# Set attention with a SwiGLU feed-forward on one core: the same instructions in another searched order

## The chip, the cores and the metric

The kernel runs on one core of a Trainium2 chip. Its engines work side by side, each through its own list of instructions in order: TensorE (PE, matmuls; PEld is its weight load), VectorE (DVE), ScalarE (ACT), GpSimd (POOL), and SyncE (SP), which here does nothing but issue transfers (DMAs). Matmul results land in one of eight PSUM banks and everything else lives in SBUF. The metric is the device time of one execution in microseconds; the figure for a kernel is the median of its runs.

## What is computed

Four batches of 12416 tokens with 128 channels. A first attention lets 32 learned vectors look at all tokens of a batch; a second lets every token look at the 32 results; the outcome goes through a root-mean-square norm and a gated feed-forward of width 1536.

```python
def mab(q, kv):
    s = scale * (q @ kv.transpose(0, 2, 1))
    s = s - s.max(-1, keepdims=True)
    a = np.exp(s)
    a /= a.sum(-1, keepdims=True) + 1e-09
    return a @ kv
h = mab(I, x)
return mab(x, h).astype(np.float32)
...
rms = np.sqrt(np.mean(x * x, axis=-1, keepdims=True) + 1e-06)
xn = x / rms * rms_g
g = xn @ w_gate
silu = g * (1.0 / (1.0 + np.exp(-g)))
val = xn @ w_val
return (silu * val @ w_out).astype(np.float32)
```

## The kernel before

**Tiling.** A batch is cut into seven sets of tokens (five of 2048, one of 1920, one of 256). The sets are cut into units of 512 tokens (480 in the sixth set, 256 in the seventh), 25 units a batch and 100 in all. A unit has 12 blocks, one for each 128 of the 1536 hidden columns: 1200 blocks.

**One block.** The token's output of the second attention is a mix of 32 vectors, so the two input products of the feed-forward are done on the 32 weights of the mix: a tile `a` of 128 rows (high, low, high, low halves of the weights) against a stack `sg` or `sv` of the 32 vectors already multiplied by `w_gate` or `w_val`. The letters are those of the order below.

- g: the gate matmul (line 655, PE). s: silu of it (line 665, ACT). v: the value matmul (line 683, PE). m: their product (line 697, DVE).
- Then the product with `w_out`, in one of three kinds. A block of kind P does it as one plain matmul p in full precision (line 753, PE, two instructions). Kinds S and D split the number in a high and a low part and use three faster matmuls: h (high part, ACT, line 710 for S, 707 for D), the low part l (line 716, DVE) for S, or n (line 723, POOL) and e (line 729, ACT) for D, then q (two matmuls, lines 741 and 742), d (the sum of both parts, line 761, POOL), and r (the third matmul, line 753).
- When a unit's 12 blocks are through: E scales up the first sum into an output buffer (line 785, ACT), F adds the second (794, DVE), T transposes (800, DVE) and O stores, as four transfers of 64 KB (line 813, SP). There are two output buffers, so E of a unit needs the store of the unit two before to have landed.

**Transfers on SP's queue.** Beside the stores: a *gather* (letter a, line 593) brings a unit's tile `a` together by four transfers of 64 KB; a *strip* (`load_channels`, line 110) loads a quarter of the channels of one set of the next batch, 256 KB in pieces of 128 bytes (32 KB for the seventh set); *rows* (`load_rows`, line 99) load one set of the next batch, four transfers; a *placement* (`place`, line 479) puts a part of a new stack in place, three transfers; `fetch` (line 458) and `put` (line 197) move weights. SP issues them strictly one after the other, and waits where one needs data or a buffer.

**The attention of the next batch** runs between the blocks of this one: strips are turned (line 300, DVE), scored (317, PE), exponentiated, summed (369, PE) and so on, each step a "micro" with a number.

**The order.** Nothing decides an order at run time. The prologue (about the first 48 us) is written out in ORDER. All that follows is in strings that an offline search wrote: `program` has one letter for each step (a dot stands for the next micro in `taken`), `picks` says which of the waiting blocks a step takes, `sorts` gives each block's kind, and `banks`, `workers`, `holders` say which buffer each result gets. Each step is emitted in that order, so the string fixes the order of every engine's own list; between engines, only data and buffers make an instruction wait.

```python
for name in "".join(program.split()):
    if name == ".":
        step, args = micros[int(next(taken))]
        step(*args)
    else:
        do[name]()
```

Of the kernel before, what the change touches and what calls it, by code (L numbers as in the profile page):

```python
# [23 lines left out]
def kernel(  # L24
# [12 lines left out]
    m = inducing.shape[0]  # L37
# [1086 lines left out]
    def seams():  # L1124
# [16 lines left out]
        0234567012456720415671260712036170236170261702367103267037127126342764132643026107243074207230427032043204235405  # L1141
        2431530523105231063506342502314217465762752615721067421074127412043413217643706423064250341530145014350231075423
        0477535436054074237037406326437603726371670527632561073607653146743674651475143261310413411271203406127654015704
        2510275140124713250152145361062102530275015617205742017451426154647626132652361253123610317562043654123742673574
        5145675360471640154012074250765172527521503565167106076754105106170647135631405316450610612064154217450465765104
        6047063710436714631062712613631734254172042104320614306120612014326042135046253035760376273657032465324763453764
        3451370163401543064216520162064506751674607643057603640345304715076013631206431046230463476140641424652014260412
        3640124651263526534253573754123657345713451350135175617210761036251036501635103650346103415317563147642714267316
        4762064201601645124564254135405364727502542304604206740634762317462317415717424571342730530132173267025723052304
        3704571475340345017430753257032734503750350375746041650160316730256736731710573463613563514364625463456147532143  # L1150
        7453253042570325637543604263476342072104720471406152076510460714273021476124716504651761261206417346724361452143
        2162570617031207507302751427043724034130132016430240145607145640714670541765146754073652043507347307235340376506
        7063065367501367163704754617563524635432164317451745067156714507410640536471357137451435132534721653762143123216
        3012346012640361503615436156415634765317650467530670346256042062305625140652165271650716506503265321562060236026
        5042012431653453425215275142710725017261275402743250327304267240720475605671403754630574307326073567326342021370
        4613064130643514210410345130724352351732513463672367526475236520365043201532613562316730563020362736470473020420
        7467354035741074645736054305436204725325305607513753051473156730163517436713512371235126031637401567013547130413
        0714107237523471246521635164312063105436024672473162307362703576025062107620516720162125710351235135013201430450
        3712543572357347632743521726746543105376453643026705674654756745074651065104527146250457641573652315421426052352
        0152017524723475307274236206706273217601467301602043207464053650325435262301051454313501345176504753050370435705  # L1160
        2704572347603504520456123053451361031401675017046720572640720627065472043640764106134017545364130140763073627160
        2357251231507234713574132737215761456421651650624652174602740741074176701731473107306742160264216401502143546513
        0425045674170450140673543145014750750251205145171460742601421624631460146321470216706401676547057154256120521542
        6415624652162345203530543275367035723576235165170527026742057624572104627407250172571520135702351025606350135203
        654135017645076514
    """
    workers = """
        2102102102102102011201021201010101012012012012112120201202020202020120120120120102101201212101201201201201201201
        201
# [5 lines left out]
        abcdefghicebjkflmadnogcbfpqrslmhjndikealcgjbpofhqmarnjpdfhgafsobdcljgprnqkamshfclnbdpgieojfrkqmalspchienofbgadrl  # L1175
        fhdqjipscnmdkoiehaqbcrjgfpnclkesmhoqcfpaernlgisbmhkeodjqpifsolakbdfpmrcshenjkqfbldpoanmrikjesgclhfqpdobsckafengr
        mdjscoqkelpabirhmcodkijlprseafhnqmsprojlbgnkqcoamedsplhfjrmgqindofeklsabmpjcnhrqgosbdkigmlenjrgqkoefhnbcsmaqrpld
        konficqjrsmpkhngreoasqlbmdnfickposqrgjmnhaeilkcgbnafdejhlmoifcdkpqserjnghobfcdelmaknqropigasjdkfalcqabmnerokpshq
        jdimbsngaekihrolfqpdjhscerdsamgcljeqobknhispfrlmcbshiejbqdarigelkpofnjbqsrmhieplkqrgbadnhoemcpjilrsnfbgkaqdmiohc
        gslmecpoknrslqfjcipmbgdraohesfbkjinprmgdbclqsaekjiclogqrdbnmsplifahbecgkqdabojsnhpclaredfbgkmhslnaigfdqporkbnmec  # L1180
        jdiqselocghkrqaenfbjkcerlgbiemqcdnpsejhfadokrlbjsgifmcbarhnedgfqjiosmkflbpigaqrnhfecomdjslknbqgclodrmnjbrcaphkmf
        ebiqnglsojrdkfebgamcpiqlmnoskhcjebgcpqbosmjclnrkipqgfemodahbrcipkesdgjrhamiceglsqdbnphcjfgaemrkobhlihqnmbesrgald
        jkmhcloefsgdiqpanrmcbejlkhnfedabisojgelmqnrkdpiscaoljqbhmdrfagnpkmbojidhfrlqscogebfinjeqpckfodibralmqsgohiedrbaq
        skplncjfmogarhlicqeskpjmfdgolnrahqcgpeobimjnrpqskdalmjnrophfqsecgbkliaprjdoqsnmehkigcolsnjfahkgbcpmrsqiejcdbfkoa
        gnhqbepilmrsfkopaqdrgelkimjfnsqobplchdkfembjikacqdnfehrsmcpgeknaoljmbhqrfdahipkgjscenofbqldaiefprmncbjkhogfsphbc
        dqmroagnjiksfperlobhniaqjmfcrkghdpsnlcmfaeohderkcqjpsbonilhmgecafbqjlrdkpmhionesdqcgbiklajpfrmeioshnkqdgarbcflhj
        moqepncgiaflkrchdbjslfpmagehcrnbjlskidfohrqpbaecfsoidhjkglpmrnqcilahnjqfkbgdmcshrqienkomplfbesrjoqpiangcfkhelqms
        jdiebcklmajfnibrcgskdqmponhegrbqdiajlpemcfskorqjbgdnifmoaphrbslqgenfrjkaidepcikmarhdobsnfgqlkjpeidmrsnakqhlopcgj
        fmebagdkshlnqbamhoeiprlgjcmfdksqniomhbljgckapfrsbqeblphfgnkirqdbomgjlesnkrcahfdgiobpqjeklhsocnmarkgflsndpbmhojcp
        ifnqarekbglmcdofsjpinhlarqgscjlomkrgnpbdjfiqsglaeokhnbdpqmjilcgdfreoiasnlbogfpadclrmhbskeijpqodafgclbjcrspkqemod  # L1190
        filhrnapjgdibqsmkloepbmjfhcdaelgqoimrjpdclsfbqgnhiemodkjrlacqnfsdkicrpbmselokfqhrgpajmdncqkirebpsldifjmgroanpqei
        bkjhlscqgacnpmkdifbrjlhcsneomlabqrkocgpsdmnlijckefpqsmnlkhdbgeijoprnaksqcfhjoipgedrhqlfncpiabgksmfjerdagpoimnfkb
        hsqrclighjprfdlekcmorasnjhdmpiqrbskdojncaflghibodskemqnphijlocbrsekadnfbgemphoqjlndersfkmhbcgopienfahdrcjsbgopkl
        mnaejqiormgbihfkbscajpnfolqmiasdnjrgecqphomflskbnarihqjdfkohnlrbsfeigpcmkdaghqrjpdbsncmoeahfqlirjkbegqihcmsrpakn
        qleomrdsfkeqarcosnkqhlroibg
# [3 lines left out]
        SDDPSSPSSPSPSPSDSSSPSSSSSSPSDPSSSDSSSDSSPSSSSSSPDSSSSPSSDSPSSSPSDPPSSSSDSSSSSSSSSSSDSPSSDSDSSSSDPSSSSDSPPSSPPSSD  # L1199
# [4 lines left out]
        PPSPPSDSDPSSPDSPSSDSPSDSDPPSSDPSSDSSSSSPSDSPDSPSSSPSPPSSPSSPSSSSDDPPPDSSSSDSSSSSPDSSSSDSSSSSPSSSPSDPDSSSPPSDSSSS  # L1204
        SSSSSDSSSPSSPDSSSSDSSSDPSPSDPPSSSPSPSDSPDSSPSPSSDPSSSDSSPSSPPSDSSSSSPPSSPDSPSDSPPPPDSSSSSSPSPPSPSSDSSPSPSSPSDSSS
        SSSSSSPSSDSDPPPSDSSPDSDPSSPSSSPSSDPSSDSPPSSPSSSSSSSPSPSSPDSSDSSSPSPSSDSSSSSSSPSSPPSSPSPSSPDSSSSSSDSPSPSSSSPSDSSS
        PDSPSDPDSSPSPSPSSSSSSPSSPSSSSSSSDSSSPPSSSDSDSSSSPSSPSDSPDPSSPSSPSPSSSSSPSSDSSPDSSPSSSPSSSSSDPSSDSPPSSPSDSSSPPSSP
        SSPSDSSSPSSPSDSSPSSSSPDSSSSSPDSSPSSDPSSDSPSPPPSPSSPSDPPSPDSSSPPSSSPSDSSSSSSSSSSS
    """
    picks = """  # L1210
        CDBCAAABBBABAABBAAAABABAAAAABAAAAAAAAAAAAAAAACACAAAAAAAACBAACAAABBAAACBAABABAAAAACABAABABBAAAABCBABAABBAAABAAAAA
        AAABAAAAAAAAAAABAAAAAAAAAAABAAAAAAAAAAAABAAAAAABAAAAAAAAAAAAABAAAAAAAAAAAAABAAAAAAAACABBBBABACAAAAAABAAAAAAAAAAA
        AAAAAABAAAAABAAAAAAAAACAAAAAAAADBABACAAAAAABBABAAAAABAABCAABAAAAAAAAAAAAABAABBBAABAACAAAABBAAABAAAAAAABAACBCDAAA
        BAACAAAAAADABADAABADABACAAABAAAAAAADABBBABABBAAABAAABBBAABABAACABBBABAAAAAAAABBAABAAAAABABAAAAAABABBAABAADAABAAA
        BBABAAAACAAACBAABBBAAABACABBBBCBAAAABAABBAABABABAAAABCBAACABAAAABAAAAAAAAABAAAAAAAABBBBBAAACAACAAABBBBAABBAAAAAA
# [234 lines left out]
```

## Time and profile before

| | |
|---|---|
| median of three runs | 1524.27 us (1522.7 to 1526.77) |
| the profiled execution | 1520.86 us, span 1518.8 us |
| mean granted clock of TensorE | 0.994 |
| DMA | 112.56 MB, 388592 packets on SP's queue, mean 74 GB/s |
| strips, from issue to landing | 5.5 us median (60 of 256 KB) |
| gathers, from issue to landing | 2.0 us median (156 + 156 of 64 KB) |

The page gives busy time by engine, 40 equal slices of the span, and the chain of work that ended last. Windows cut the span where one likes and give busy time by engine in each; the timeline lists instructions in order of time, with neighbours of one form merged; the waits say who waited for whom. The costliest groups on PE, DVE and POOL (busy time, mean of one, idle time before):

```profile
L655 PE MATMUL gv<-a,sg 128*128 128x512 f32 (+2 forms) x1188 | 507.4, 428 | 12.3 <-DMA a<-lo 9.2
L697 DVE TENSOR_TENSOR gv<-silu,gv 128x512 f32<-128x512 f32 (+2 forms) x681 | 445.5, 668 | 15.8 <-ACT silu L665 7.7
L761 POOL TENSOR_TENSOR u<-xn,u 128x512 fp32r<-128x512 f32 (+2 forms) x327 | 401.6, 1239 | 10.9 <-PE gv L742 10.1
```

Matmuls are pipelined, so their durations overlap and the sum of a group is more than the time that it holds PE; the chain's shares are the better price.

### The profile page before, as it was taken

The numbers are of one execution on the slowest core, as the hardware profiler recorded it, in microseconds if no ns is written. First come the engines' busy times: TensorE is split into PE (matmuls) and PEld (weight loads), VectorE is DVE, ScalarE is ACT, GpSimd is POOL, SyncE is SP. The second block draws the span as 40 slices with busy tenths as digits, with TensorE's granted clock in tenths as the row PEclk, the third lists the DMA queues.
The fourth block names the chain that finished last, engine by engine and source line by source line (L and its number), as shares of the span: only waits on it lengthen the run. The fifth ranks groups of instructions, "written<-read, shape, count | busy, mean of one in ns | idle before, by whom it ended". The sixth has DMA issues, their size and how long they took to land.

```text
span 1518.8 us, 26130 instructions
## 1 busy us (share of the span) xinstructions
PE 1492.1 (98%) x7198; PEld 1107.9 (73%) x7198; DVE 1454.5 (96%) x2572; ACT 1327.1 (87%) x2748; POOL 1426.9 (94%) x1351
## 2 busy tenths in 40 slices
PE   9998999999999999999989999999999999999998
PEld 6556677777776777776768776777678777777786
DVE  6998999999999999999979999999999999999998
ACT  5797899898898889988879888989899989899896
POOL 1497999999999999999989999999999999999998
PEclk9999999999999999999999999999999999999999
DMA  7584225532755213736573222264222112212222
GB/s 290 81 114 85 45 55 124 129 78 49 105 94 98 38 30 63 149 73 108 90 128 62 48 42 43 43 137 100 43 40 43 31 36 42 35 36 43 42 41 34
DMA packets 389329, 112.56 MB, mean 74 GB/s; under 512 B 365088, under 2 KB 369728, under 8 KB 386624
## 3 DMA queue, kind: packets, MB, share of 16 engines
q1 hardware_dynamic: 388592, 110.83, 38.3%
q8 instruction: 57, 0.93, 0.3%
q14 instruction: 88, 0.72, 0.2%
q10 hardware_dynamic: 592, 0.08, 0.0%
HBM read 53.95 MB, written 27.00 MB: 53 GB/s over the span
## 4 chain that ended last, share of the span: by engine, by line
PE 92%; SPq 3%; DVE 2%; ACT 1%; DMA 1%; issue 1%; POOL 0%; DVEq 0%; ACTq 0%; POOLq 0%
PE gv L753 28%; PE gv L655 17%; PE gv L683 16%; PE gv L741 12%; PE gv L742 12%; PE gv L317 3%; SPq L110 2%; PE gv L526 1%; PE gv L369 1%; PE gv L854 1%; DMA a<-lo 1%; SPq L593 0%; DMA xT<-in_x_dram 0%; ACT silu L665 0%; PE gv L153 0%
## 5 line engine op out<-in xcount | busy, mean ns | idle before, releaser
L665 ACT ACTIVATE silu<-gv 128x512 f32<-128x512 f32 (+2 forms) x1193 | 686.4, 590 | 105.8 <-PE gv L655 73.4
L655 PE MATMUL gv<-a,sg 128*128 128x512 f32 (+2 forms) x1188 | 507.4, 428 | 12.3 <-DMA a<-lo 9.2
L697 DVE TENSOR_TENSOR gv<-silu,gv 128x512 f32<-128x512 f32 (+2 forms) x681 | 445.5, 668 | 15.8 <-ACT silu L665 7.7
L683 PE MATMUL gv<-a,sv 128*128 128x512 f32 (+2 forms) x1188 | 455.8, 409 | 4.3 <-ACT o L785 4.3
L761 POOL TENSOR_TENSOR u<-xn,u 128x512 fp32r<-128x512 f32 (+2 forms) x327 | 401.6, 1239 | 10.9 <-PE gv L742 10.1
L761 POOL TENSOR_TENSOR xn<-xn,xn 128x512 fp32r<-128x512 f32 (+2 forms) x309 | 384.9, 1255 | 4.8 <-PE gv L742 4.1
L710 ACT ACTIVATE xn<-gv 128x512 fp32r<-128x512 f32 (+2 forms) x598 | 345.7, 587 | 26.4 <-DVE gv L697 18.8
L697 DVE TENSOR_TENSOR u<-silu,gv 128x512 f32<-128x512 f32 (+2 forms) x512 | 335.6, 665 | 10.3 <-PE gv L683 4.5
L753 PE MATMUL gv<-u,wo 128*128 128x512 f32 (+1 forms) x648 | 326.0, 587 | 0.2
L655 PEld LDWEIGHTS gv<-a,sg 128*128 128x128 f32 x1188 | 225.0, 190 | 121.6 <-issue 31.4
L683 PEld LDWEIGHTS gv<-a,sv 128*128 128x128 f32 x1188 | 223.9, 189 | 96.4 <-issue 21.2
L716 DVE SCALAR_TENSOR_TENSOR xn<-xn,gv 128x512 fp32r<-128x512 f32 (+2 forms) x330 | 216.6, 661 | 7.9 <-ACT xn L710 6.5
L716 DVE SCALAR_TENSOR_TENSOR u<-xn,gv 128x512 fp32r<-128x512 f32 (+2 forms) x268 | 172.9, 650 | 2.1 <-ACT xn L710 0.9
L761 POOL TENSOR_TENSOR xn<-xn 128x512 fp32r<-128x512 f32 (+2 forms) x131 | 164.9, 1262 | 5.7 <-PE gv L742 4.8
L741 PE MATMUL gv<-xn,xn 128*128 128x512 f32 (+2 forms) x400 | 153.8, 385 | 0.0
L723 POOL TENSOR_TENSOR xn<-u,xn 128x512 fp32r<-128x512 f32 (+2 forms) x110 | 138.4, 1262 | 7.4 <-ACT xn L707 5.2
L761 POOL TENSOR_TENSOR u<-u 128x512 fp32r<-128x512 f32 (+2 forms) x109 | 137.2, 1262 | 1.1 <-PE gv L655 0.7
L753 PEld LDWEIGHTS gv<-u,wo 128*128 128x128 f32 x648 | 120.4, 190 | 23.8 <-issue 7.9
L741 PE MATMUL gv<-xn,more 128*128 128x512 f32 (+2 forms) x344 | 136.0, 395 | 0.0
L707 ACT ACTIVATE xn<-u 128x512 fp32r<-128x512 f32 (+2 forms) x169 | 104.9, 622 | 4.8 <-DVE u L697 3.2
L729 ACT ACTIVATE xn<-xn 128x512 fp32r<-128x512 f32 (+2 forms) x169 | 104.7, 627 | 4.2 <-POOL u L723 2.1
L753 PE MATMUL gv<-u,xn 128*128 128x512 f32 (+2 forms) x253 | 97.5, 395 | 0.1
(215 smaller groups left out, 2359.5 us busy)
## 6 DMA issues: line engine op xcount, KB each, us to landing
out_dram<-o SPq DMA_DIRECT2D x320, 64.0 KB, 2.1
xT<-in_x_dram SPq DMA_DIRECT2D x60, 256.0 KB, 5.5
xn<-in_x_dram SPq DMA_DIRECT2D x60, 256.0 KB, 5.5
a<-hi SPq DMA_DIRECT2D x156, 64.0 KB, 2.0
a<-lo SPq DMA_DIRECT2D x156, 64.0 KB, 2.0
xn<-in_x_dram SPq DMA_DIRECT2D x5, 1024.0 KB, 9.0
xn<-w SPq DMA_DIRECT2D x18, 256.0 KB, 4.3
out_dram<-o SPq DMA_DIRECT2D x64, 60.0 KB, 2.0
```

What stands on the lines that cost most here:

```text
L655: nc.tensor.matmul(g[:, 0:T], stacks[b][0][:, ts(j, P)], halves_in_turn(one["a"][:, 0:T]), start=True, stop=True)
L665: nc.scalar.activation(sl[:, 0:T], gates.pop(n)[:, 0:T], AF.Silu)
L683: nc.tensor.matmul(v[:, 0:T], stacks[b][1][:, ts(j, P)], halves_in_turn(one["a"][:, 0:T]), start=True, stop=True)
L697: nc.vector.tensor_tensor(out=to, in0=sl[:, 0:T], in1=v[:, 0:T], op=ALU.mult)
L707: nc.scalar.activation(hi, t["u"], AF.Copy, scale=1.0 - 2.0 ** -13)
L710: nc.scalar.activation(hi, t["u"], AF.Copy, scale=-(1.0 - 2.0 ** -13) * 2.0 ** -12)
L716: nc.vector.scalar_tensor_tensor(out=t["lo"], in0=t["hi"].bitcast(F32), scalar=4096.0, in1=t["u"], op0=ALU.mult, op1=ALU.add)
L723: nc.gpsimd.tensor_tensor(out=t["lo"], in0=t["u"], in1=t["hi"].bitcast(F32), op=ALU.subtract)
L741: nc.tensor.matmul(to, weight_of(0, j), halves_in_turn(t["hi"]), start=not one["q"], stop=False)
L742: nc.tensor.matmul(to, weight_of(1, j), halves_in_turn(t["lo"]), start=False, stop=last)
L753: nc.tensor.matmul(to.rearrange("p (n h) -> p h n", h=2) if step2 else to, lhsT, rhs, start=one["left"] == NJ, stop=one["left"] == 1)
L761: nc.gpsimd.tensor_tensor(out=t["lo"], in0=t["hi"].bitcast(F32), in1=t["lo"].bitcast(F32), op=ALU.add)
```

## The change

Only strings change: `banks`, `workers`, `holders`, `sorts`, `picks`, `program` and `taken` are replaced by those of another search. `outputs`, the functions and the prologue stay. The multiset of numbers in `taken` is the same, so the same micros run. Ten of the 1200 kinds differ (counts in the prediction). The description given with the change: same instructions in another searched order, found with transfers that share a server and strip loads that hold up the next issue. The diff, cut to the first lines of the order and the kinds:

```diff
     sorts = """
...
-        SDDPSSPSSPSPSPSDSSSPSSSSSSPSDPSSSDSSSDSSPSSSSSSPDSSSSPSSDSPSSSPSDPPSSSSDSSSSSSSSSSSDSPSSDSDSSSSDPSSSSDSPPSSPPSSD
+        SDDPSSPSSPSPSPSDSSSPSSSSSSPSDPSSSDSSSDSSPSSSSSSPDSSSSPSSDSPSSSPSSPPSSSSDSSSSSSSSSSSDSPSSDSDSSSSDPSSSSDSPPSSPPSSD
...
     program = """
-        ...g.gs....g.v.vsgmgs.gm.vsvvmsg..ms.mvsv.p....gp..s..mgp....v.sm.p...gmp...g.v.g.vspm..p.s.mgv.v.v.p.sm.gsmghgm
-        p..s....hvp..s.p.s.vmgvgm..smhg..nps..gnlvspem.v.vqe.gsqmdvvEmagsgm.vsrmvsgqmhdvpmshlgd.p.l.smv.ghpm...h.vsv.pl.
-        .hm.r.gl...hFs.l...n.gqmsg.vd..gsqmevv.sdq.hgmqs.m..E.hgd.v.s.m....rvrl.p...lqhdr..qgm..dsl.r.v.gdq.vsgmvqsd.mvh
...
+        ........ggs.vvs.vgmgs.vg.m.vgsm.s.mmvg..v.g.p.s.p...s.pms.g.sm.v..gp.s...pm..gps..v.v..pm.mgps....vgv.mv.gsmg.pm
+        h......gv..ph.v.s.psmsgvm..hm.g..nps.sgnlv.gpem.eqvs.qsvmdgEvgmsaqmg.svrvmsgvm.vspdm...hpmhdlph..h.vlg.psl..gmr.
+        sl..F.hg...vgsnvmg..s..hm..sl.q..v..r.gq.sdmvgevmgh.d.s.msv..ghvqms..d..l..r.glq.r.qh.dq.gl..E.dqs.qmrdvp..sdgmv
...
     taken = """
-        1 54 5 41 55 80 0 9 56 2 3 110 57 42 4 113 6 43 10 17 44 7 114 18 11 107 13 12 45 14 108 46 19 15 109 47 25 59
...
+        5 0 9 80 54 1 41 55 81 2 3 56 110 57 42 43 109 11 10 6 17 12 44 7 108 13 45 18 19 4 14 114 46 25 15 47 21 59 107
...
```

Read out as SP's queue, the places that the prediction speaks of are these. The number ahead is how much PE work, in us, stands before the entry in the order (how it is priced is in the prediction); "room" is how much stands between a gather and the first gate that reads it. A strip is named by batch, set and quarter, a store and a gather by batch and unit, both counted from 0; "s6" is the small seventh set.

```
before                                     after
30.2 strip 1,2,2   31.0 strip 1,1,1        24.4 strip 1,1,1   28.8 strip 1,2,0
32.3 strip 1,3,1   34.3 strip 1,3,0        31.6 put           32.0 strip 1,2,2
35.7 strip 1,3,2   37.3 strip 1,s6,1       34.9 strip 1,2,1   36.9 put
38.1 strip 1,4,1   39.3 put                36.9 strip 1,s6,1  37.1 strip 1,5,1
39.6 strip 1,s6,3  40.0 strip 1,1,0        39.3 strip 1,4,3   41.3 strip 1,5,2
41.7 strip 1,5,0   42.9 strip 1,2,0        42.9 strip 1,5,3   44.5 strip 1,2,3
43.5 strip 1,5,3   44.5 strip 1,4,0        46.5 strip 1,s6,2  47.1 strip 1,5,0
45.9 strip 1,4,2   47.1 strip 1,2,1        49.2 put
48.4 strip 1,s6,0  49.0 strip 1,5,1        49.8 store 0,0     51.8 store 0,1
50.4 strip 1,2,3   52.2 strip 1,5,2        54.4 gather 0,4, room 4.2
52.6 store 0,0
55.4 gather 0,4, room 3.8

306.7 to 314.6 seven strips                307.5 store 0,18   309.5 strip 2,s6,3
315.8 store 0,19   319.5 store 0,20        311.5 store 0,19
321.2 strip 2,5,2  322.0 strip 2,s6,2      314.8 gather 0,23, room 12.9
322.8 gather 0,23, room 4.5

368.3 gather 1,2, room 11.2                369.6 strip 2,3,0  371.6 rows 2,s6
                                           373.4 strip 2,2,2  375.8 gather 1,2, room 3.7

672.1 store 1,19   674.4 store 1,20        671.1 strip 3,1,1  673.4 rows 3,1
677.0 strip 3,4,1  678.0 rows 3,1          675.2 strip 3,3,3
680.4 strip 3,s6,2 680.4 strip 3,2,3       679.8 placement    681.7 store 1,20
681.9 rows 3,0     683.9 placement         686.9 gather 1,24, room 5.1
685.8 strip 3,3,3
687.1 gather 1,24, room 4.9

884.2 rows 3,3     885.9 rows 3,2          883.8 rows 3,2     885.7 rows 3,3
899.0 rows 3,5                             887.5 store 2,10
900.3 gather 2,14, room 4.1                889.6 gather 2,14, room 13.8
```

## The prediction

> **What bounds the kernel now.** I read the page first: busy shares, the 40 slices and the chain of waits.
>
> ```profile
> span 1518.8 us, 26130 instructions
> PE 1492.1 (98%) x7198; PEld 1107.9 (73%) x7198; DVE 1454.5 (96%) x2572; ACT 1327.1 (87%) x2748; POOL 1426.9 (94%) x1351
> PE   9998999999999999999989999999999999999998
> PE 92%; SPq 3%; DVE 2%; ACT 1%; DMA 1%; issue 1%; POOL 0%; DVEq 0%; ACTq 0%; POOLq 0%
> ```
>
> The end is set by the matmuls (PE), and behind PE there is only the SP queue, which issues the transfers. Three slices of PE fall below 9 in the middle or at the end. So next I cut the span where PE pauses (columns: window, its length, busy time and count of each engine, granted clock, DMA share, GB/s).
>
> ```profile
> 60.00:71.00 11.00, 9.51 (x27) 4.73 (x26) 9.29 (x17) 8.17 (x16) 4.74 (x4) 1.00 0.78 74
> 115.50:127.00 11.50, 6.43 (x17) 4.29 (x16) 6.88 (x11) 6.16 (x12) 4.80 (x5) 0.70 0.84 145
> 127.00:404.00 277.00, 276.82 (x1371) 203.69 (x1371) 272.88 (x475) 248.22 (x506) 273.44 (x251) 1.00 0.43 80
> 404.00:413.00 9.00, 6.47 (x29) 5.00 (x28) 6.74 (x14) 6.49 (x18) 6.67 (x9) 1.00 0.63 105
> 413.00:780.00 367.00, 366.98 (x1775) 273.98 (x1773) 359.49 (x630) 330.44 (x686) 362.61 (x343) 1.00 0.46 84
> 780.00:798.00 18.00, 12.45 (x43) 9.10 (x42) 9.94 (x17) 9.68 (x25) 11.05 (x14) 0.82 0.97 147
> 798.00:1004.00 206.00, 205.98 (x1003) 153.18 (x1005) 202.74 (x358) 186.57 (x379) 202.55 (x186) 1.00 0.29 53
> 1004.00:1014.00 10.00, 8.91 (x47) 6.47 (x40) 9.96 (x19) 7.55 (x16) 10.00 (x10) 1.00 0.62 146
> 1014.00:1478.00 464.00, 463.40 (x2050) 354.94 (x2049) 455.72 (x781) 418.18 (x872) 458.41 (x432) 1.00 0.25 47
> ```
>
> The four long windows are 1314 us and PE lacks 0.18 + 0.02 + 0.02 + 0.60 = 0.82 us in them: there the order is already tight. The five short windows hold what can be won. Call them A (60), B (115.5), C (404), D (780) and E (1004): PE is idle in them for 1.49, 5.07, 2.53, 5.55 and 1.09 us. In B and D the granted clock falls as well (0.70, 0.82). The timeline shows how: from 122.9 to 125.9 us matmuls of 512 columns start 0.43 us apart instead of 0.215, and from 792.7 to about 798.4 those of 480 columns 0.40 instead of 0.20. Half speed over 5.1 us of work in B and 5.7 us in D is another 2.5 and 2.9 us. After the idle 2.53 us of C the clock stays at 1.00.
>
> The waits (total, times, longest) and then the SP queue's timeline (start, time taken, line, count) name the cause.
>
> ```profile
> PE gv L655 <- DMA a<-lo: 9.2, 3, 5.5
> PE gv L683 <- ACT o L785: 4.3, 1, 4.3
> ACT o L785 <- DMA out_dram<-o: 7.3, 2, 6.4
> ```
>
> ```profile
> 85.09 9.99 SPq L110 DMA_DIRECT2D xT<-in_x_dram  x7
> 95.18 1.49 SPq L197 DMA_DIRECT2D w<-xn  x1
> 96.71 17.82 SPq L110 DMA_DIRECT2D xT<-in_x_dram  x12
> 114.64 3.56 SPq L813 DMA_DIRECT2D out_dram<-o  x4
> 118.30 0.57 SPq L593 DMA_DIRECT2D a<-hi  x1
> ```
>
> In B, 19 strip loads (L110) sit in front of the first store. Twelve in a row cost 17.82 us, 1.485 each, though a lone one costs 0.59 (at 409.00). The store starts at 114.64, the scale-up L785 that must reuse its buffer waits 6.4 us, and the value matmul behind waits 4.3. C, D and E are gates (L655) whose gather came late. A is DVE held by a strip (1.59 us) ahead of the subtraction L491 that a gate needs.
>
> **The change, part by part.** The work hardly changes. Ten kind letters differ: 685 S, 191 D and 324 P become 688, 187 and 325. PE gives up one block of three matmuls (3 × 0.21) for two plain halves (2 × 0.43 at 512 columns): +0.2 us. DVE gains 3 × 0.68 = 2.0, POOL loses 5 × 1.29 = 6.5, and ACT 4 × 0.61 plus 1 × 0.61 = 3.1 us; PE covers all three, and they are too small to turn one of them into the bound. Everything else is order: 84 strips, 21 row loads of four issues each, 97 gathers of four and 100 stores of four, as before.
>
> To compare the orders I give each SP entry a **position**: the PE work ahead of it, at the chain's prices. Shares of 16.8, 16.2, 11.8 + 11.7 and 28.2% over 1200 gates, 1200 values, 876 pairs and the rest are 0.213, 0.205, 0.408, 0.204 (a third) and 0.77 us (a plain block). Attention matmuls get 1.8, 1.0, 2.0 or 0.3 by their runs in the chain. Both orders total 1385. The unit is about 1.04 us, (1518.8 − 54 − 21) / 1385.
>
> *B.* Before, the strips from position 30.2 on keep SP busy from 85.09 to 114.53, and the store is due at 52.6, 22.4 × 1.04 = 23.3 us after the first: 108.4. It is 6.2 us late, as the 6.4 us wait says. After, 12 strips and three puts stand between 24.4 and the store at 49.8: at most 12 × 1.485 + 3 × 1.49 = 22.3 us of issuing in 25.4 × 1.04 = 26.4. The first store is on time. What is late next is the gather of unit 4, behind two stores: room 4.2, need 3.9 (three issue steps of 0.63 and 2.0 to land). With stores at the crowded 3.56 us each and strips at 1.49 it is 5.4 late, with the median prices of the L110 and L813 rows (0.67 and 4 × 0.505) it has 0.4 to spare. That is priced below.
>
> *A.* The strip that DVE waited for moves from the sixth strip to the second, position 8.9 to about 4: −1.49.
>
> *C.* The gather of batch 0's unit 23, at position 322.8 with room 4.5, stood behind seven strips (11.62 us in the timeline), two stores (7.13) and two more strips. Now it stands at 314.8 behind two stores and two strips of the small last set, and its room is 12.9: −2.53.
>
> *D.* Two stores, four strips, eight row loads and a placement stood in the 15 units before the gather at 687.1; SP was busy from 767.15 to 784.71 and then one gather issue alone took 3.85 us. Now one placement and one store stand in the last 11 units: −8.4.
>
> *E.* Twelve row-load issues (17.16 us, 1.43 each) ended at 1006.07 and the gather at position 900.3 was late, with room of 4.1. It moves up to 889.6 with room 13.8, behind eight of them and a store, 15.0 us of issuing at crowded prices from position 883.8: 8.9 late at most, plus 3.9 for itself, inside 13.8 × 1.04. −1.09.
>
> Saved: 1.5 + 7.6 + 2.5 + 8.4 + 1.1 = 21.1 us.
>
> *New tight places.* I walk SP's entries in order, each starting at its position or when the one before is done. Crowded prices make the new gathers late as follows: unit 4 of batch 0 by 5.4, unit 2 of batch 1 by 3.9 (its room falls from 11.2 to 3.7), and units 15, 21, 3 of batch 1 and 15 of batch 0 by 1.6, 1.1, 1.0 and 1.1; the rest stay under 1. By median prices none is over 0.3 late. The same walk over the old order gives 10.8 (D), 9.5 (B), 4.7 (C), 4.0 (E), and 5.4 and 5.0 at two gathers where PE did not stop. Of these 39.4 us, 14.2 showed as idle PE, a share of 0.36. On the new sum of 14.1 that is 5.1; since nothing showed at 5.0 and 5.4, and the low end is 0, I take 4, and 14.1 as the upper end. Time spent queued at crowded prices, summed over all entries, falls from 895 to 460.
>
> A late gather stops PE because gates run in order: behind it stand the values, and behind them silu, L697 and the POOL adds. Whether 5 us more brings the half clock, no row between 2.53 (no) and 5.07 (yes) decides; so the two worst get 2.9 each at the upper end. The Trainium skill (TensorE: Matmul & The Clock Gate, What's actually happening) puts the fall after about one idle window of 3.4 us; by it, unit 4 and unit 2 at their crowded lateness would each pay it, which is the upper end already named.
>
> Net: 0.2 − 21.1 + 4 = −16.9. On the profiled execution's 1520.86 (2.06 outside the span) this is 1504.0. That execution lies 3.41 below the median of the runs, so **1507**. Ends: returns of 0 give 1503, returns of 14.1 + 5.8 = 19.9 give 1523.
>
> **Rivals.** *Strips on the same rings.* Three new gathers directly follow a strip (1.2 to 2.4 units behind): units 2 and 21 of batch 1, unit 2 of batch 2. The longest landing of a gather is 6.9 against 2.0. If all three suffer these 4.9 us beyond their small spare room, the time is 1507 + 3 × 4.0 = 1519. For it: the 3.85 us issue in D, behind a strip. Against: lone strips stand before gathers in the old order too, without a wait. The Trainium skill (DMA: Bandwidth & Descriptors, Queues, rings and completion order) says that each DMA engine takes descriptors in ring order, which would make a gather wait for a strip's data; this is that rival.
>
> *Slower: thinned rooms.* Eight gathers fall from 8 to 13.5 of room to under 5 (batch 1: 2, 3, 6, 21; batch 2: 1, 2; batch 3: 23, 24). If issue and landing take 5 us above 3.9, as where a strip blocked the issue, four of them in batches 1 and 2 become stalls like D: 4 × 8.4 − 21.1 + 4 gives 1541; from three it is slower than before. Against: the old order has 20 gathers with room under 5, as many as the new, and only those with a backlog stopped PE.
>
> *The stalls go, the tight stretches loosen.* 1314 us at 0.06% loss is a property of this order. If the new one loses 1% there, 13 us come back: 1520. Distances between producer and consumer of a block (gate to silu, multiply to high, add to third) have the same medians and first percentiles within 0.2 in both orders, so I doubt it.
>
> *Early DMA supply.* DMA is over 1 busy from 90 to 115; if B only moves later, 7.6 returns: 1515.
>
> **How the numbers follow.** Forecast 0.68; rings 0.08; slower 0.07; looser 0.09; supply 0.08. About 0.3% (4.6 us) is what a measurement of this kernel tells from no change: faster means below 1519.7. The forecast's own range is 1501 to 1515. Adding rings, supply and most of looser gives 1501 to 1520. Faster: 0.68 + 0.08 + half of rings and of looser 0.08 = 0.84; same 0.09; slower 0.07.
>
> **What would show it.** Right: PE idle between 100 and 1478 below 6 us, no window with a clock under 0.95 there, L785's wait on the store gone, the strips at 85 us in small groups. Wrong: a wait of L655 on a gather above 3 us, at unit 4 of batch 0 (near 115 us) or unit 2 of batch 1 (near 450); or PE lacking more than 0.3% in the stretches without transfers.

## The result and the profile after

The changed kernel takes 1503.84 us (median of 4 runs, 1503.3 to 1504.27) against 1523.57 (four runs, 1522.7 to 1526.77) before: a ratio of 0.9867, interval 0.9849 to 0.9884. Its profiled execution took 1504.27 us; the forecast on that scale was 1504.0, and 1507 for the median.

The page of the changed kernel, the same four lines as before:

```profile
span 1502.5 us, 26083 instructions
PE 1488.1 (99%) x7197; PEld 1101.2 (73%) x7197; DVE 1454.4 (97%) x2575; ACT 1324.6 (88%) x2743; POOL 1419.8 (94%) x1346
PE   8999999999999999999999999999999999999998
PE 91%; DVE 3%; ACT 2%; DMA 2%; issue 1%; SPq 1%; POOL 0%; ACTq 0%; DVEq 0%; POOLq 0%
```

The span is 16.3 us shorter and PE's busy time 4.0 (1492.1 to 1488.1), so its idle time fell by 12.3. In the chain SP's queue has gone from 3% to 1%, and in the slices no dip is left between the prologue and the end. The same kind of windows, shifted a little since the new order runs ahead of the old one:

```profile
60.00:71.00 11.00, 10.57 (x33) 5.63 (x31) 10.64 (x19) 9.95 (x20) 6.52 (x6) 1.00 0.84 116
115.50:127.00 11.50, 11.50 (x49) 8.93 (x48) 10.67 (x19) 10.92 (x23) 11.14 (x10) 1.00 0.80 124
127.00:404.00 277.00, 276.01 (x1366) 201.71 (x1365) 272.12 (x474) 247.07 (x507) 271.00 (x253) 1.00 0.46 86
404.00:413.00 9.00, 9.00 (x42) 7.66 (x41) 8.75 (x16) 7.82 (x21) 8.98 (x12) 1.00 0.14 30
413.00:770.00 357.00, 356.20 (x1717) 262.13 (x1716) 346.67 (x608) 318.35 (x658) 350.22 (x326) 1.00 0.45 84
770.00:790.00 20.00, 20.00 (x97) 16.10 (x98) 19.89 (x42) 17.64 (x48) 20.00 (x24) 1.00 0.48 83
790.00:990.00 200.00, 199.64 (x967) 146.66 (x966) 196.39 (x341) 181.15 (x366) 195.93 (x181) 1.00 0.34 60
990.00:1004.00 14.00, 14.00 (x61) 10.90 (x60) 13.81 (x26) 10.85 (x24) 13.65 (x14) 1.00 0.42 89
1004.00:1462.00 458.00, 457.71 (x2025) 349.91 (x2024) 451.69 (x776) 413.23 (x860) 452.16 (x425) 1.00 0.24 47
```

B, C, D and E are gone to the last hundredth: PE is busy for the whole of 115.5 to 127, 404 to 413, 770 to 790 and 990 to 1004, and the granted clock is 1.00 there. What is left lies in the long windows, 0.99 + 0.80 + 0.36 + 0.29 = 2.44 us in 1292, where the old order lacked 0.82 in 1314.

The SP timeline of the changed kernel at B (start, time taken, line, count):

```profile
84.70 3.37 SPq L110 DMA_DIRECT2D xT<-in_x_dram  x2
88.17 1.07 SPq L197 DMA_DIRECT2D w<-xn  x1
89.34 11.50 SPq L110 DMA_DIRECT2D xT<-in_x_dram  x8
100.95 2.03 SPq L197 DMA_DIRECT2D w<-xn  x1
105.69 5.34 SPq L813 DMA_DIRECT2D out_dram<-o  x8
111.13 0.57 SPq L593 DMA_DIRECT2D a<-hi  x1
```

and PE's timeline just behind, with the longest wait of a gate for a gather in the whole execution (in brackets the idle time before the matmul and who ended it):

```profile
115.19 0.45 PE L655 MATMUL gv<-a,sg 128*128 128x512 f32 x1 [0.40 <-DMA a<-lo]
```

The longest run of strips is 8 instead of 12, and 2.7 us lie free ahead of the first store, which starts at 105.69 instead of 114.64. Here both units' stores go out as one row of eight, and the gather of unit 4 behind them costs PE 0.40 us, not the 5.4 of crowded prices. The remaining stops over 0.3 us are of the same size: 0.73 at 49.9 (DVE), 0.59 at 291.5 (a silu, L665), 0.68 at 621.7 (the scale-up L785 behind a store), 0.36 at 801.8 (a gather).

### The profile page after: what moved, and what is told of

Same layout as the page of the kernel before. It is cut to its first block, busy times and chain, and to the rows that moved or that the text cites. A ratio compares the mean times of both kernels' runs of the same rounds, so it can differ in the third digit from the quotient of the medians.

```text
span 1502.5 us, 26083 instructions
## 1 busy us (share of the span) xinstructions
PE 1488.1 (99%) x7197; PEld 1101.2 (73%) x7197; DVE 1454.4 (97%) x2575; ACT 1324.6 (88%) x2743; POOL 1419.8 (94%) x1346
## 4 chain that ended last, share of the span: by engine, by line
PE 91%; DVE 3%; ACT 2%; DMA 2%; issue 1%; SPq 1%; POOL 0%; ACTq 0%; DVEq 0%; POOLq 0%
PE gv L753 29%; PE gv L683 16%; PE gv L655 16%; PE gv L741 12%; PE gv L742 11%; PE gv L317 3%; PE gv L526 1%; PE gv L369 1%; ACT silu L665 1%; DMA out_dram<-o 1%; PE gv L854 1%; DMA xn<-in_x_dram 1%; DVE gv L697 1%; PE gv L463 0%; DMA a<-lo 0%
## 5 line engine op out<-in xcount | busy, mean ns | idle before, releaser
L665 ACT ACTIVATE silu<-gv 128x512 f32<-128x512 f32 (+2 forms) x1193 | 681.8, 590 | 90.9 <-PE gv L655 68.2
L655 PE MATMUL gv<-a,sg 128*128 128x512 f32 (+2 forms) x1188 | 503.7, 424 | 3.2 <-DMA a<-lo 0.8
L683 PE MATMUL gv<-a,sv 128*128 128x512 f32 (+2 forms) x1188 | 463.8, 412 | 0.1
L761 POOL TENSOR_TENSOR u<-xn,u 128x512 fp32r<-128x512 f32 (+2 forms) x308 | 380.0, 1245 | 4.1 <-PE gv L742 3.5
L761 POOL TENSOR_TENSOR xn<-xn,xn 128x512 fp32r<-128x512 f32 (+2 forms) x300 | 374.3, 1257 | 5.3 <-PE gv L742 5.0
L697 DVE TENSOR_TENSOR u<-silu,gv 128x512 f32<-128x512 f32 (+1 forms) x509 | 331.9, 664 | 7.3 <-PE gv L683 2.6
L753 PE MATMUL gv<-u,wo 128*128 128x512 f32 (+2 forms) x650 | 324.6, 585 | 0.2 <-DVE u L697 0.2
L655 PEld LDWEIGHTS gv<-a,sg 128*128 128x128 f32 x1188 | 224.2, 189 | 110.1 <-issue 24.4
L683 PEld LDWEIGHTS gv<-a,sv 128*128 128x128 f32 x1188 | 223.8, 189 | 94.9 <-issue 15.7
L716 DVE SCALAR_TENSOR_TENSOR xn<-xn,gv 128x512 fp32r<-128x512 f32 (+2 forms) x346 | 225.3, 656 | 5.8 <-ACT xn L710 3.6
L761 POOL TENSOR_TENSOR xn<-xn 128x512 fp32r<-128x512 f32 (+2 forms) x149 | 184.4, 1244 | 4.7 <-PE gv L742 3.6
L716 DVE SCALAR_TENSOR_TENSOR u<-xn,gv 128x512 fp32r<-128x512 f32 (+2 forms) x241 | 155.6, 651 | 2.1 <-ACT xn L710 1.0
L761 POOL TENSOR_TENSOR u<-u 128x512 fp32r<-128x512 f32 (+2 forms) x118 | 147.5, 1253 | 1.0 <-PE gv L742 0.9
L753 PEld LDWEIGHTS gv<-u,wo 128*128 128x128 f32 x650 | 120.6, 189 | 28.5 <-issue 11.4
L723 POOL TENSOR_TENSOR xn<-u,xn 128x512 fp32r<-128x512 f32 (+2 forms) x103 | 130.0, 1265 | 4.8 <-ACT xn L707 4.3
L753 PE MATMUL gv<-u,xn 128*128 128x512 f32 (+2 forms) x240 | 91.5, 387 | 0.0
```

What stands on the lines that cost most here:

```text
L655: nc.tensor.matmul(g[:, 0:T], stacks[b][0][:, ts(j, P)], halves_in_turn(one["a"][:, 0:T]), start=True, stop=True)
L665: nc.scalar.activation(sl[:, 0:T], gates.pop(n)[:, 0:T], AF.Silu)
L683: nc.tensor.matmul(v[:, 0:T], stacks[b][1][:, ts(j, P)], halves_in_turn(one["a"][:, 0:T]), start=True, stop=True)
L697: nc.vector.tensor_tensor(out=to, in0=sl[:, 0:T], in1=v[:, 0:T], op=ALU.mult)
L716: nc.vector.scalar_tensor_tensor(out=t["lo"], in0=t["hi"].bitcast(F32), scalar=4096.0, in1=t["u"], op0=ALU.mult, op1=ALU.add)
L723: nc.gpsimd.tensor_tensor(out=t["lo"], in0=t["u"], in1=t["hi"].bitcast(F32), op=ALU.subtract)
```

## The experiments

The theory of the prediction is that the order of SP's loads among the stores and gathers made the stops, so that the compute work's new order is worth nothing by itself. Each experiment takes one of the two orders as its base and moves transfers alone; its whole edit is in `program` (the place of a dot or of an `a`) and `taken`. The diffs show the first lines that differ. Stops are PE's idle times in the middle of the run, and a "slow period" is a stretch in which the trace shows the clock granted at one half.

**1. The old order with only the loads moved to the new places** (84 strips and 21 sets of rows).

```diff
-        ...g.gs....g.v.vsgmgs.gm.vsvvmsg..ms.mvsv.p....gp..s..mgp....v.sm.p...gmp...g.v.g.vspm..p.s.mgv.v.v.p.sm.gsmghgm
+        ...g.gs....g.v.vsgmgs.gmv.svvmsg..ms.mvsv.p....gp...s.mgp...v.sm.p..g.mp..g.v.g.vsp.m..p.s.mgv.v.v..p.sm.gsmghgm
...
```

> The order of before, with nothing moved but the strips and row loads of the next batch, each to the position that it has in the order after (stores, gathers and all compute stay where before has them). If SP's queue alone makes the difference, stalls A, B, C, E go and D shrinks (the walk at crowded prices leaves the gather of batch 1 unit 24 5.1 late instead of 10.8): 1524 - 21 + 3 to 6 = 1506 to 1509, and no window at half clock. If the gain comes from the new interleaving of compute, or from the gathers' and stores' own places, it stays above 1516.

Measured: 1514.6 us (1511.41 to 1516.87), ratio 0.9934 (0.9915 to 0.9952), with 1525.36 for the kernel before on that chip. A half of the gain, and neither theory's number. A to E had gone; three other stops of over 2 us had come, of 2.26 us at 128.5, 3.28 at 526.6 and 2.10 at 826.8. The waits of this kernel around 520 to 532:

```profile
PEld gv L655 <- DVE xn L716: 4.5, 2, 4.1
DVE xT L300 <- DMA xT<-in_x_dram: 4.4, 1, 4.4
```

The turn L300 waits for a strip, DVE stands still, and the gate behind it on PE lacks the block that DVE should have freed. At the two other stops a turn waits for a strip as well, for 3.0 and 2.5 us. The cause is in the code: the turn of a set's first quarter already reads all four strips of the set. In the old compute order the new places leave some strips only 0.7 to 4.5 us of work ahead of that first turn, where the landing alone takes 5.5. So loads fit only an order whose turns come late enough.

**2. The new order with the loads put back to the old places.**

```diff
-        ........ggs.vvs.vgmgs.vg.m.vgsm.s.mmvg..v.g.p.s.p...s.pms.g.sm.v..gp.s...pm..gps..v.v..pm.mgps....vgv.mv.gsmg.pm
+        ........ggs.vvs.vgmgs.vg..mvgsm.s.mmvg.v..g.p.s.p....spms.g..sm.v..gp..s..p.m..gps..vv..pm.mgps...vgv.mv.gsmg.pm
...
```

> The order after, with only the strips and row loads moved back to before's positions. If SP's queue alone makes the difference, the stalls near the gathers of batch 0 unit 4 and batch 1 unit 24 come back with their half clock (walk: 16.8 and 11.8 late, a share of 0.36 to 0.5 of it as idle PE): 1504 + 14 to 22 = 1518 to 1526. If the compute order carries the gain: below 1510.

Measured: 1526.7 us (1524.87 to 1528.97), ratio 1.0009 (1.0 to 1.0019): the whole gain is lost, and the time lies 0.7 us above the slow end of what was expected. The window at B:

```profile
108.00:130.00 22.00, 9.53 (x26) 5.02 (x28) 8.15 (x14) 9.32 (x15) 9.29 (x8) 0.69 0.80 133
```

and this kernel's waits in it:

```profile
DVE xT L300 <- DMA xT<-in_x_dram: 13.8, 2, 12.8
PE gv L655 <- DVE u L697: 12.5, 1, 12.5
```

PE is idle for 12.47 us in one piece, again behind a turn that waits for its strips, and a slow period of 13.65 us goes with it. Two gates that waited for their gathers are the smaller part, 1.50 us at 442.8 and 2.52 at 799.2, the second with a slow period of 3.41. So the new compute order gains nothing with the loads in the old places, but most of the loss here is a fault that the old order with these places does not have. That the loads' places carry the gain is shown by experiment 6.

**3. D alone**: in the old order seven loads that stood close ahead of the gather of batch 1's unit 24 (five strips, two sets of rows) go to their new places: two strips behind that gather, the other five further ahead of it.

```diff
-        809 419 334 810 426 811 812 813 814 815 335 817 356 344 816 357 345 428 421 414 346 418 368 439 436 369 417 818
+        809 419 334 810 426 811 812 813 814 815 335 817 356 344 816 357 345 428 421 424 414 346 418 368 439 436 369 447
...
```

> The order of before, with only the seven loads ahead of the gather of batch 1 unit 24 (five strips, eight row-load issues) moved to their positions in the order after. Theory: stall D goes with its half clock, 5.55 + 2.9 = 8.4 us, less 0 to 1.5 for what stays late there (3.8 at crowded prices): 1515 to 1517. If the fall of the clock has another cause than the idle PE, only 5.5 us go: 1518 to 1519. If the loads only stall another place: 1522 or more.

Measured: 1515.58 us (1514.62 to 1518.71), ratio 0.9939 (0.9923 to 0.9954): 9.8 us off 1525.36. The window of D, which had 12.45 busy of 18 at a clock of 0.82:

```profile
780.00:798.00 18.00, 18.00 (x86) 14.52 (x85) 17.67 (x35) 16.30 (x42) 18.00 (x21) 1.00 0.69 108
```

D's stop is caused by what SP issues close ahead of that gather, and its price of 8.4 lies within the interval of the ratio, 7 to 12 us.

**4. B alone, to the new places**: the 19 strips ahead of the first store.

```diff
-        21 60 26 81 20 58 27 61 22 23 28 33 48 30 34 137 29 49 35 50 31 62 51 136 52 53 63 36 37 38 39 69 74 64 65 79 66
+        21 60 26 81 20 58 27 111 61 22 23 28 33 48 30 34 137 29 49 35 50 31 62 51 136 52 53 63 36 37 38 39 112 69 74 64
...
```

> The order of before, with only the 19 strips ahead of the first store moved to their positions in the order after. Theory: stall B goes with its half clock, 5.07 + 2.5 = 7.6 us, and little of it returns at units 5 and 6 (4.1 and 3.7 late at crowded prices): 1516 to 1518. If the early DMA traffic is the limit and not the queue's order, the stall only moves: 1521 or more.

Measured: 1522.63 us (1520.37 to 1525.37), ratio 0.9982 (0.9973 to 0.9991): a miss, and the number that the rival, the early transfers as such, had named. Experiment 5 decides between them. The windows of B and of what follows:

```profile
115.50:127.00 11.50, 11.50 (x47) 8.45 (x46) 11.49 (x20) 11.24 (x23) 11.50 (x10) 1.00 0.67 133
127.00:145.00 18.00, 15.37 (x55) 10.43 (x54) 14.03 (x25) 12.72 (x29) 13.99 (x15) 0.91 0.55 93
```

and, of this kernel's waits between 128 and 140 us, the longest:

```profile
DVE xT L300 <- DMA xT<-in_x_dram: 3.5, 1, 3.5
```

The store is on time and B is gone, but 7 us later the turn waits for a strip, with its own 2.39 us stop and a slow period of 3.41. It is experiment 1's fault in small. (The trace is of the slowest of the ten runs, 1525.37 us; in it A, at 2.70 us, and C, at 2.79, have slow periods as well.)

**5. B alone, with leads kept**: the same 19 strips, each at least 15 us of PE work ahead of the first turn of its set.

```diff
-        .hm.r.gl...hFs.l...n.gqmsg.vd..gsqmevv.sdq.hgmqs.m..E.hgd.v.s.m....rvrl.p...lqhdr..qgm..dsl.r.v.gdq.vsgmvqsd.mvh
+        l..hm.r.gl...hFs...l..n.gq.msgvd..gsqmev.vsdq..hg.mqs.m.E.hgd.v.sm....rv.r.lp....lq..hdr..qgm..dslr.vgdq.vsgmvqs
...
```

> The kernel before with only the 19 strips that stood ahead of the first store moved, not to the changed kernel's places as in b_only_B but to those of b_loads_spread, each at least 15 us of PE work ahead of the first turn of its set. Theory: b_only_B gained only 2.7 us because its strips came late for the first turn, not because the stop at 119 us is worth nothing; with leads kept the stop goes and none takes its place: the stop of 5.07 us and some of the half clock behind it, 5 to 9 us under the kernel before of this call, 1515.5 to 1519. Rival: the delay is only passed on, whichever way the strips are placed: at least 1521, with a stop of 2 us or more between 110 and 150 us.

Measured: 1517.66 us (1516.52 to 1519.75), ratio 0.997 (0.9959 to 0.9982), 4.8 us off 1522.49; inside the expected time, a little short of the expected gain. No stop is left from 115 to 145:

```profile
115.50:127.00 11.50, 11.50 (x45) 8.16 (x44) 11.49 (x20) 11.24 (x23) 11.50 (x10) 1.00 0.66 138
127.00:140.00 13.00, 13.00 (x55) 9.76 (x54) 12.96 (x24) 12.50 (x29) 12.78 (x13) 1.00 0.47 71
```

A part may have gone back at A: two of the strips now stand 19 and 38 us of work earlier, ahead of it, and the stop at 69.0 us is 3.69 long, with a slow period of 3.41 behind it. The longest wait of a turn there, in the same kernel's waits from 66 to 74 us:

```profile
DVE xT L300 <- DMA xT<-in_x_dram: 3.9, 1, 3.9
```

How much of that is the strips' doing is not shown: in experiment 3, where nothing near A moved, the stop at A was 2.28 us long with a slow period of 3.41 too, against 1.38 without one in the trace of the kernel before. The stop at B and the missing lead were two separate faults, and curing one must not make the other.

**6. The loads spread by two rules.** In each of the two orders the strips and rows were placed anew so that, by the walk along SP's queue at crowded prices, few gathers come late and every strip stands at least 6 us ahead of the first turn of its set. Nothing else is touched (99 loads move in the old order).

```diff
-        ...g.gs....g.v.vsgmgs.gm.vsvvmsg..ms.mvsv.p....gp..s..mgp....v.sm.p...gmp...g.v.g.vspm..p.s.mgv.v.v.p.sm.gsmghgm
+        ...g.gs....g.v.vsg.mgs.gm.vsvvmsg..ms.mvsvp....gp..s.mgp...v.sm.p...gmp...g.v.g.vspm..p.s.mg.v.v.v.p..sm.g.smgh
...
-        h......gv..ph.v.s.psmsgvm..hm.g..nps.sgnlv.gpem.eqvs.qsvmdgEvgmsaqmg.svrvmsgvm.vspdm...hpmhdlph..h.vlg.psl..gmr.
+        ....gv..ph.v.s.psmsg.vm..hm.g..nps.sgnlv.gpem.eq.vs.qsvmdgEvgmsaqmg.svrvmsgvm.vspdm..hp.mhdlph..h.vlg.p.sl..gmr.
...
```

(The second pair is of the new order.)

> The order of before, with only the strips and row loads moved, this time spread so that the walk at crowded prices has no gather more than 3.5 us late and every strip stands at least 6 us ahead of the first turn of its set, which reads all four strips (b_loads_as_after had left leads of 0.7, 1.6, 2.7 and 4.5 there). If SP's queue alone carries the gain: 1505 to 1511, and no wait of DVE on a strip above 1.5 us. If the compute order after is worth something by itself, it stays at 1513 or more.

> The order after, with the strips and row loads spread by the same rule. Only 0.40 + 0.36 us of idle PE at late gathers and 0.59 at a late store are left for it to win in the order after: 1502.5 to 1505, no difference that can be told. Above 1507 would say that the walk at crowded prices is no guide where there is no backlog left.

Measured on one chip: the old order 1501.87 us (1501.16 to 1502.38), ratio 0.9855 (0.9833 to 0.9877); the new order 1503.73 (1503.65 to 1505.18), ratio 0.987 (0.9851 to 0.9889). The old compute order, with nothing but its loads moved, does at least as well as the changed kernel, and 3 us better than the theory's range. The new one gains nothing from other places, as expected.

The one stop above 0.4 us left in the old order after the prologue is 2.22 us at 326.7. Its cause, in the SP timeline of the old order so spread:

```profile
320.04 1.97 SPq L99 DMA_DIRECT2D xn<-in_x_dram  x4
322.11 2.62 SPq L813 DMA_DIRECT2D out_dram<-o  x4
324.78 1.89 SPq L479 DMA_DIRECT2D sv<-whi  x3
```

and in its PE timeline:

```profile
328.90 0.48 PE L683 MATMUL gv<-a,sv 128*128 128x512 f32 x1 [2.22 <-DVE z L532]
```

Four row loads stand ahead of a store, the store ahead of a placement, and DVE's L532 needs the placement's data. A rule for gathers and strips alone hadn't looked at placements.

**7. That stop cured**, with the changed kernel and the uncured order as yardsticks on the same chip: one entry, the rows, goes behind the next gathers.

```diff
-        247 249 248 242 366 250 649 650 260 651 652 167 653 155 654 655 168 656 657 156 658 659 191 145 660 179 661 662
+        247 249 248 242 250 649 650 260 651 652 167 653 155 366 654 655 168 656 657 156 658 659 191 145 660 179 661 662
```

> The order of b_loads_spread with one entry moved: the four row loads of set 6 for batch 1, which there stood just ahead of a store (320.04 us, 1.97 us of issue) and pushed back the last three weight loads of the next pair behind that store (324.78), go to just behind the next pair of gathers. Theory: PE's only stop over 0.4 us in b_loads_spread (2.22 us at 326.7, ended by DVE z L532, which waited for the sv load) goes, nothing else does: 1.5 to 2.5 us under b_loads_spread on the same chip, 1498.5 to 1500.5. Rival: the wait only goes somewhere else (the weight loads are late because of the stores, or the rows now hold a gather): within 0.8 us of b_loads_spread, with another stop of about 2 us in the trace.

> The order of b_loads_spread unchanged, beside the changed kernel on one chip. Theory: the loads' places alone carry the gain, and the spread places are a little better than those of the change: 1501 to 1503, and 1 to 3 us under the changed kernel of this call. Rival: the 1.9 us between the two medians so far came from the chips: within 0.8 us of the changed kernel here.

> The changed kernel as it is, as the yardstick of this call: 1503 to 1505 by every theory.

Measured: cured 1500.16 us (1499.73 to 1500.43), ratio 0.9854 (0.9838 to 0.9869); uncured 1501.71 (1501.36 to 1501.92), 0.9864 (0.985 to 0.9877); changed kernel 1503.75 (1503.07 to 1503.98), 0.9877 (0.9863 to 0.989). The three sets of runs don't overlap, so the two differences, 1.55 and 2.04 us, are of the orders and not of the chips. The cured kernel, the fastest of all here, has this on its SP timeline:

```profile
318.68 2.61 SPq L813 DMA_DIRECT2D out_dram<-o  x4
321.33 1.89 SPq L479 DMA_DIRECT2D sv<-whi  x3
```

and this on its page:

```profile
span 1498.2 us, 26134 instructions
PE 1486.0 (99%) x7198; PEld 1107.8 (74%) x7198; DVE 1452.5 (97%) x2572; ACT 1325.2 (88%) x2748; POOL 1425.1 (95%) x1351
PE 97%; DVE 1%; ACT 1%; issue 0%; SPq 0%; DMA 0%; POOL 0%; DVEq 0%; ACTq 0%; POOLq 0%
```

The placement goes out at 321.33 instead of 324.78 and the stop is gone; the longest one left is 0.98 us at 422.8, at a gather. PE's busy time is 2.1 us below the changed kernel's: besides its few stops, the changed kernel has matmuls that hold PE longer in sum than those of the old order.

**8. Gathers with their room taken away**: in the new order 14 gathers of batch 3 move to 0 to 1.8 us of work ahead of the first gate that reads them.

```diff
-        dmaqsglrhrvmdsvrlrhrgmhdqvmrrpFdhlhqslgnqslgvvsmvdgeqmsgTqdsrmqhOvhmgdvrslrgqmsdgalqsvmghqdmrsrv.gdpmshlphdlhgvl
+        dmqsglrhrvmdsvrlrhrgmhdqvmrrapFdhlhqslgnqslgvvsmvdgeqmsgTqdsrmqhOvhmgdvrslrgqmsdglqsvmghqdmrsrv.gdpmshlphdlhgvlr
...
```

> The order after, with 14 gathers of batch 3, where no loads run, moved down to 0 to 1.8 us of PE work ahead of their first gate. Each should stop PE for 3.9 - 1.04 x room, so six stops near 3.9, three near 3.3, five of 2.0 to 2.8, in sum up to 45 us. What the traces have shown so far of the clock: no half speed after stops of 1.71 or less, always after 3.28 or more, either way from 2.1 to 2.8. By that, nine or more half-speed periods of 3.41 or 6.83 us, each costing half its length: 1504 + 45 + 15 to 35 = 1560 to 1584. If a stop has to fill a whole period of 3.41 us, at most a few: 1550 to 1556.

Measured: 1509.1 us (1508.83 to 1510.27), ratio 0.9905 (0.9886 to 0.9924). Both theories failed: 13 of 14 gathers cost nothing, and one made the only new stop, 3.65 us at 1429.3 with a slow period of 6.83 behind it. The SP timeline there, first of this kernel:

```profile
1405.53 0.51 SPq L593 DMA_DIRECT2D a<-hi  x1
...
1410.05 18.82 SPq L813 DMA_DIRECT2D out_dram<-o  x8
1428.98 0.51 SPq L593 DMA_DIRECT2D a<-hi  x1
```

and in the changed kernel:

```profile
1406.27 0.51 SPq L593 DMA_DIRECT2D a<-hi  x1
...
1410.79 1.95 SPq L813 DMA_DIRECT2D out_dram<-o  x4
1419.77 0.51 SPq L593 DMA_DIRECT2D a<-hi  x1
...
1427.65 1.95 SPq L813 DMA_DIRECT2D out_dram<-o  x4
```

Where the gather only moved past compute work, it was issued as early as before (1405.53 against 1406.27). One was moved past the next store as well. That store waits for its output until about 1427, SP waits with it (18.82 us for the row of eight), and the gather starts at 1428.98 instead of 1419.77.

## Why the prediction was right, and where it was off

**The direction and its cause** held. A gather or a store was late because SP was still busy with loads; a better order of the loads removes that (experiment 3 for D, 5 for B, 6 for the whole; C and E were not tested alone).

**Saved.** B, C, D and E were priced at 7.6, 2.5, 8.4 and 1.1 us; all of their 14.24 us of idle time and 5.1 of half clock are gone. (5.4 was forecast. The two slow periods last 6.83 us each, PE is idle for 2.43 of B's and 1.09 of D's, and half of the rest is 2.2 and 2.9; B has 4.4 us of work at half speed and not 5.1.) The single tests gave 9.8 for D (interval about 7 to 12, from the ratio) and 4.8 for B, the latter with a loss at A in it. A was mis-sized: 1.49 forecast, and from 48 to 100 us PE's idle time fell from 1.91 to 1.39, 0.52. Moving the strip removed a part of the wait, and DVE is late elsewhere (0.73 at 49.9).

**E's cause was misread.** The prediction took its twelve row loads for 17.16 us of issuing, 1.43 each. In the old kernel's trace eight of them go out between 988.9 and 992.5 us, 0.42 each, nothing until 1004.37, and then the last four in 1.7 us; a line of the timeline counts such pauses in. In between SP waits, at the end for the last matmul of line 369, which ends at 1004.31 and which by the code reads such a row buffer. In SP's waits of the whole old execution this is the longest one of the line:

```profile
SPq L99 <- PE gv L369: 26.0, 5, 8.4
```

So E's gather stood behind a load that was itself waiting, which is the fault that experiment 8 makes with a store. The new order has the gather ahead of those four row loads; the 1.09 us were saved, but not by shorter issuing, as the price had it.

**Returned.** 4 us were taken for new tight places. From 100 to 1478 us PE is idle for 2.83 us, of which 0.81 was there before in the long windows: 2.0 came back. Unit 4 of batch 0 returned 0.40 and unit 2 of batch 1 nothing. Crowded prices, 5.4 and 3.9, overstate them.

**PE's work** was put at +0.2 us. Busy time less the half clock rose by 1.1 (−4.0 + 5.1). Traces without a slow period in the middle show PE busy for 1486.0 to 1486.5 us in the old compute order (three traces) and 1487.9 to 1490.1 in the new one (three). From the start of a matmul to the start of the next, idle time taken off, the value matmuls (L683) hold PE for 302.3 us in the changed kernel and 296.3 in the cured old order, L317 for 49.7 and 47.9; L753, L655 and L463 give back 2.3, 1.4 and 1.6. The ten kinds don't explain it; that the lines have other neighbours may, but no run shows it.

**The sum** on the profiled execution: idle −14.24 (B to E) − 0.52 (A) + 2.0 (returned) + 0.42 (prologue +0.70, end −0.28) = −12.3, half clock −5.1, work +1.1: −16.3 of span against the forecast −16.9. A, the half clock, the work and the prologue came out 2.6 us worse than forecast, the returns 2.0 better. So the sum is closer than its terms. The prologue's 0.70 need not be an effect of the change: its idle time lies between 4.6 and 6.2 us in the traces of either order.

**The 3 us between 1507 and 1503.84** come from a step that isn't in the sum: the 3.41 us by which the old kernel's profiled execution lay under its median were carried over to the new one, whose profiled execution lies 0.43 above its median. We take the offset to belong to the stops. The old order's runs, in this and the later comparisons, lie between 1520.5 and 1527.7, those of the changed kernel between 1503.1 and 1504.3. C shows how a stop scatters: 2.53 us without a slow period before, 2.59 without one in experiment 3, 2.46 with 3.41 in experiment 5, 2.79 with 6.83 in experiment 4. That the old kernel's own median is made so is argued from these, since only one of its executions has a trace.

**The walk's rule for the start of an entry** (at its position, or when the one before is done) is wrong where positions come from the compute work: SP doesn't see compute work, only the entries ahead of it and what each one waits for (experiment 8). It worked here, as we read it, because in this change the gathers' neighbours on the queue changed too. It also lacked a demand: a strip must lie a landing ahead of the first turn of its set (experiments 1 and 4). The new order met that demand, so the lack cost the forecast nothing, but it would have misjudged both experiments' orders.

**The rivals.** *Rings*: over the whole execution gates waited for gathers 0.8 us in two pieces, neither at the three units named; behind a strip they came in time. *Thinned rooms*: none of the eight stopped PE by more than 0.40, and experiment 8 shows that room counted in PE work says little by itself. *Looser stretches* was right in sign only: the long windows lose 0.19% instead of 0.06%, 1.6 us and not 13. *Early supply*: the window of B is full, at a DMA share of 0.80, so the delay was the order on SP's queue and not the transfers' sum.

**What was to show it** did: 2.83 us idle where less than 6 was named, no clock under 0.95 in any window, strips in runs of at most 8. L785's wait on the store at B went too, though one of 2.3 us came elsewhere, ending at 287.9 us, ahead of the stop of 0.59 at 291.5.

## What to carry to other kernels

On a queue that issues in order, ask of each urgent transfer what stands ahead of it on that queue alone, at the price of a crowded run, and whether one of those waits for data or a buffer (E, experiment 8); and ask of each load that is moved which first reader needs it (here a turn that reads four strips at once). When stops go, their half-clock periods and the scatter of the runs go with them: cost the median from a trace without the stops and don't carry the old offset over. A searched order can hide a small loss in its main work behind a large gain in its waits, so move the waiting part alone before adopting the whole.

## What the hardware showed unexpectedly

**The half clock goes by fixed windows of 3.41 us.** In the traces of these kernels its periods in the middle of the run last 3.41, 6.83 or 13.65 us, once, twice and four times 3.41. Within one execution their starts lie a whole number of such windows apart: 197 in the old kernel, 19, 99 and 212 behind the first in experiment 4. So one can lay the windows over an execution and add up PE's idle time in each. Of the 15 periods 14 begin at the end of a window with at least 2.11 us idle, and no other window outside a slow period has more than 1.86. The one exception is experiment 1's stop of 3.28 us, which lies in two windows with 1.74 and 1.66 idle. By this, stops of 2.53 us (C before) and 2.59 (C in experiment 3) brought no slow period, split as they were in 1.37 and 1.16 and in 1.01 and 1.59, while one of 2.28 (A in experiment 3), in a single window, did. All 15 periods ended with the first window that had 0.30 us idle or less; 0.68 or more kept them on. The steps agree with the free-running window of 3413 ns that the Trainium skill gives (TensorE: Matmul & The Clock Gate, What's actually happening). Its table, in which the clock falls after at least one idle window of about 3.4 us, does not: here 2.28 us without a matmul were enough. The price of a stop of 2.3 to 2.8 us is therefore itself plus 0, 1.7 or about 3.1 us, by how it lies in the windows.

**One issue can take seven times its usual time.** In the changed kernel the first issue of a gather, behind eight row loads and a store, took 4.04 us (0.58 is usual):

```profile
607.68 3.56 SPq L99 DMA_DIRECT2D xn<-in_x_dram  x8
611.35 3.69 SPq L813 DMA_DIRECT2D out_dram<-o  x4
615.93 4.04 SPq L593 DMA_DIRECT2D a<-hi  x1
```

Before, the like at 785.58 took 3.85, behind row loads, a placement and a strip. It isn't the gather's own: a store's first issue at 460.38 in the old kernel took 3.50, a placement's at 764.89 in the changed one 4.17. Each of the four stands a few entries behind row loads, most of which took 0.42 us, so the delay can show at a later issue, whoever that is for. Why it falls just there, no run shows.

The store in this row shows a second kind of wait. Its issues take 0.3 to 0.4 us, but the last three start at 612.35, 613.52 and 614.73, just when the row loads eight entries ahead have landed (612.33, 613.51, 614.71). Each entry counts its landing on one of eight semaphores (the counters on which engines wait) and here waits until the entry that had it before has landed, so no more than eight of these transfers are on their way at once. The gather's delay stayed covered. The store landed at 621.60, the scale-up L785 began at 621.74, and PE's stop of 0.68 us at 621.7 ended behind it, at 622.39.
